# A build-time scheduler's table of priorities: the first six head pairs, the first MLP and the groups of decoded weights get numbers of their own

## The chip, the core and the metric

The kernel runs on one core of a Trainium2 chip. Its work is shared by the TensorE (PE in the profile; PEld is its weight load), VectorE (DVE), ScalarE (ACT), GpSimd (POOL) and SyncE (SP, which here issues most of the DMAs). The metric is the device time in microseconds. The time before is the median of three runs; one further execution was profiled, and every time of an instruction below comes from that one.

## The reference

Attention over 8 batches of 8 heads, and on its output a gated MLP with a product along the sequence. All is fp32.

```python
# q, k, v: (8, 8, 576, 64)
q_rot, k_rot = rotate(q), rotate(k)              # rotary positions
scores = (q_rot @ k_rot.T) / sqrt(64)
attn = exp(scores - max(scores))
out = (attn / (sum(attn) + 1e-9)) @ v
x = out.transpose(0, 2, 1, 3).reshape(8, 576, 512)
h = maximum(x @ w_in, 0)                         # w_in: 512 x 1024
u, v = h[..., :512], h[..., 512:]
v_n = (v - mean(v)) / sqrt(var(v) + 1e-6)
gated = u * (w_spatial @ v_n + b_spatial)        # w_spatial: 576 x 576
result = gated @ w_out                           # w_out: 512 x 512
```

## The kernel before, in words

**Units of work.** Two heads of one batch are a pair; there are 32 pairs, four to a batch. After the pairs 4b to 4b+3 comes the MLP of batch b. Large products are done in several passes with a high and a low part of each operand.

**A pair.** `prepare(i)` loads q and k as `st<i>_0` and `st<i>_1` and applies the rotary positions: two products of 128x576 with the table `tab2` and a sum, on POOL for most pairs (L563, L578). From pair 4 on ACT then scales the k half (`st<i>_1`, L652), DVE makes its low part `lk` (L540), ACT and POOL make `hq` and `lq`, and SP copies all of it by DMA into the stacks `ks`, `qs` and `qz` that the score matmuls read (L429). There is one set of stacks, so those of pair i+1 can be written only when the tiles of pair i that read them are through. `attention(i)` makes nine score tiles `sc<i>_<c>` in the order 0, 1, 2, 3, 8, 4, 5, 6, 7 (four or six matmuls of 288 columns each, L750); DVE takes the negated maximum (`nmx`, L760), ACT the exponential `e` with its sum (L761), DVE transposes it (`tu`, L771), and PE multiplies with v in three pieces of 96 small matmuls (`pv`, L715). `normalise` divides (`rb`, L825, L826) and makes the parts of `x`.

**An MLP.** PE runs `pa` (the v half of the first product, L874), `pb` (the u half, L897), `pc` (along the sequence, L915) and `pd` (the output, L935). `norm` is the normalisation, `gate` the product with u. The weights arrive as 64-bit words and are made into floats by `decode`, once, during the first pairs.

**What sets the order.** Every step is handed to `Program` with the engine it runs on, an estimated length, what it reads and writes, and a sort key. `Program.run` walks through a simulated time at build: whenever an engine is free it takes the ready step with the smallest key, if the buffers that the step opens can be had from their pools (two score tiles `sc`, four `pm` for the MLP's products, four `e`, four `stage`, ...). What comes out is one fixed order of instructions for each engine; on the chip each engine works through its own in order and waits where data isn't there. Where PE would find nothing before 200 us of that simulated time, `warm` matmuls on zeros are put in. The key of a step is 20 times its pair's number (or 80 times its MLP's, plus a start) and an offset from the tables at the top of the file:

```python
PREP = [...]     # offsets of a pair's preparation: load, rope, sum, hi, lo, stacks
STAGE = [...]    # scores, step, max, exp, turn, chunk, values
NORM = [...]     # inverse, fetch, x, its parts
DEC_ON = -60.279479                   # the later steps of a weight's decoding
K_LOAD, K_ROPE, K_SUM, K_HIQ, K_LOQ, K_LOK, K_STACK, K_STACK2 = PREP_E if i < FIRST else PREP
```

`PREP_E`, `STAGE_E` and `NORM_E` hold for the first six pairs together (`FIRST = 6`). An offset thus moves a kind of step against all others, on its engine, without touching what the step does.

Of the kernel before, what the change touches and what calls it, by code (L numbers as in the profile page):

```python
# [22 lines left out]
HF = DFF // 2  # L23
# [6 lines left out]
PE, ACT, DVE, POOL, DMA = "pe", "act", "dve", "pool", "dma"  # L30
# [8 lines left out]
}  # L39
PSUM = {"sc": 1024, "pm": 512}  # L40
MOE_START, MOE_LENGTH = 94.478379, 78.548222
DEC_V = [97.949631, 82.361107, 593.702782, 288.768656]
DEC_S = [84.682668, 152.53349, 99.527247]
DEC_U = [-568.813081, -65.866382, -0.431134, 175.381419]
# [31 lines left out]
K_LATE = 163.209501  # L76
UNTIL = -5282.532269
LATE_LOAD = 300
SOON = 108.92456
FIRST = 6  # L80
PREP = [-848.367164, -374.753764, -69.9844, -244.721214, -617.60192, -1064.500205, 581.882473, -475.784363]
PREP_E = [51.687636, 298.661164, 17.879536, 140.254064, -184.884171, 639.680467, 73.636456, 484.33577]
PREP_AT = [-441.032351, -69.597063, -819.530327, -30.251418, -111.190708, 107.347515]
STAGE = [-7.255147, 1.255075, -127.272341, -353.119135, 244.349862, 3.682899, 10.320485]
STAGE_E = [-17.885167, 1.413295, -324.778667, -335.590414, -18.444203, 500.740646, 14.840595]
ATT_AT = [-7.442792, -9.232278, -6.449832, 1.846545, -111.323694, -67.478676]
NORM = [-413.12016, 513.410815, -713.32848, 231.181969, -280.547004]
NORM_E = [-178.78421, 267.172514, -208.498036, -240.944501, -239.600932]
MOE0 = [106.701094, 81.129356]
# [15 lines left out]
def pool_ns(n):  # L105
    return 160 + n * 32 // 15
# [21 lines left out]
class Program:  # L128
# [5 lines left out]
    def op(self, eng, ns, key, f, r=(), w=(), new=(), port=False, late=0):  # L134
        return self.either({eng: ns}, key, lambda e: f(), r, w, new, port, late)
# [171 lines left out]
def tile_attention_gated_mlp(  # L307
# [11 lines left out]
    nc = tc.nc  # L319
# [23 lines left out]
    op = prog.op  # L343
# [90 lines left out]
    def rest_lo(eng, lo, src, hi):  # L434
        eng.tensor_tensor(out=lo, in0=src, in1=hi.bitcast(F32), op=ALU.subtract)  # L435
# [4 lines left out]
    def decode(key, where, at, src, after=()):  # L440

        n = f"w{'io'[where is wout]}" + "".join(map(str, at))
        tiles = {}
        sg = Buf("m", [P, HF], I32, f"sg{n}")
        tok = ("raw", n)
        ts = nc.vector.tensor_scalar
        stt = nc.vector.scalar_tensor_tensor

        def word(j, dt=None):
            w = tiles["raw"][:, :, j]  # L450
            return w.bitcast(dt) if dt else w
# [392 lines left out]
    def mlp(b):  # L844
        x = xs[4 * b:4 * b + 4]
        pm_pools = "pm"
        start, length = (MOE_START, MOE_LENGTH) if b else MOE0
        base = 80 * b + start
        spent = [0]
        whole = (4 * 12 + 8) * pe_ns(HF) + (16 * 12 + 8 * 14) * pe_ns(HALF)  # L850
# [52 lines left out]
        for f in range(4):  # L903
            fs = slice(f * P, (f + 1) * P)
            for c in range(2):
                pm = Buf(pm_pools, None, None, f"pc{b}_{f}{c}")
                cc = slice(c * HALF, (c + 1) * HALF)
                for t in range(NQ):
# [87 lines left out]
    def gate(u, g, c, pm, key, done):  # L996
# [113 lines left out]
```

## Time and profile before

| what | value |
|---|---|
| median of 3 runs | 897.56 us (893.99 to 898.61) |
| profiled execution: time, and span from its first to its last instruction | 891.51 us, 889.7 us |
| mean granted clock of PE | 0.992 |
| PE busy, matmuls | 858.7 us, 97% of the span |
| PE busy, weight loads | 757.9 us, 85% |
| DVE / ACT / POOL busy | 580.6 us (65%) / 497.5 us (56%) / 511.2 us (57%) |
| share of the chain that ended last: PE / DMA / "issue" | 65% / 11% / 9% |

PE's busy time counts the modelled ends of pipelined matmuls and also a matmul that runs at half clock. So the idle time between groups of weight loads (PEld) is the better place to see PE wait. The profiled execution's own time is 6.05 us below the median.

### The profile page before, as it was taken

The page shows a single profiled execution, that of the slowest core. Times are in us where ns is not written, and L with a number is a line of the kernel's source. Part 1 is how long each engine was busy: PE and PEld are TensorE (multiplying, and loading weights), DVE is VectorE, ACT ScalarE, POOL GpSimd, SP SyncE. Part 2 cuts the span into 40 slices and gives each one's busy share as a digit, 9 for nine tenths or more (in the row PEclk, how much of TensorE's full clock was granted, in tenths as well). Part 3 has the DMA queues.
Part 4 walks back from the last instruction along what each step waited for, and adds up shares of the span by engine and source line. Part 5 has one row for each costly group of instructions (what it writes and reads, how often), then busy time and mean ns, then how long its engine had stood idle before and what let it go on. Part 6 is the DMA issues. An engine that isn't in the chain of part 4 may idle for free.

```text
span 889.7 us, 32677 instructions
## 1 busy us (share of the span) xinstructions
PE 858.7 (97%) x13709; PEld 757.9 (85%) x13709; DVE 580.6 (65%) x1169; ACT 497.5 (56%) x1239; POOL 511.2 (57%) x509
## 2 busy tenths in 40 slices
PE   9999989988999999999999999999999999999998
PEld 7666668878878998889979988899978998899898
DVE  6787788747577665857678565857687665855120
ACT  2665578635448545754558445755567555753442
POOL 7666699766357665566457664566557664312121
PEclk9998899999999999999999999999999999999999
DMA  9977646778888888877888788878987888552101
GB/s 195 246 231 188 146 104 150 174 166 190 211 175 187 189 182 213 190 175 173 210 204 193 171 179 211 186 173 187 224 200 176 187 197 205 121 115 53 54 1 55
DMA packets 99622, 150.88 MB, mean 170 GB/s; under 512 B 30929, under 2 KB 46929, under 8 KB 99474
## 3 DMA queue, kind: packets, MB, share of 16 engines
q1 hardware_dynamic: 98962, 148.12, 71.6%
q8 instruction: 108, 1.77, 0.9%
q10 hardware_dynamic: 512, 0.66, 0.3%
q14 instruction: 40, 0.33, 0.1%
HBM read 94.24 MB, written 9.88 MB: 117 GB/s over the span
## 4 chain that ended last, share of the span: by engine, by line
PE 65%; DMA 11%; issue 9%; SPq 4%; DVE 4%; POOL 4%; ACT 2%; POOLq 0%; DVEq 0%; ACTq 0%
PE sc L750 15%; PE pv L715 11%; PE pc L915 11%; PE pb L897 9%; PE pa L874 7%; PE pd L935 5%; DMA st<-in_qk_dram 4%; PE warm L1009 4%; SPq L429 3%; DMA ks<-st 2%; POOL st L563 2%; PE pr L616 1%; DMA vr<-in_v_dram 1%; DVE tu L771 1%; DVE nmx L760 1%
## 5 line engine op out<-in xcount | busy, mean ns | idle before, releaser
L760 DVE TENSOR_REDUCE nmx<-sc 128x1 f32<-128x576 f32 x288 | 211.5, 740 | 133.5 <-PE sc L750 131.2
L761 ACT ACTIVATE e<-sc,nmx 128x576 f32<-128x576 f32 x288 | 212.5, 739 | 144.7 <-DVE nmx L760 142.5
L771 DVE STREAM_TRANSPOSE tu<-e 128x576 f32<-128x576 f32 x288 | 216.5, 762 | 17.7 <-ACT e L761 9.7
L563 POOL TENSOR_TENSOR st<-st,tab 128x576 f32<-128x576 f32 x112 | 157.8, 1429 | 58.2 <-DMA st<-in_qk_dram 43.5
L715 PE MATMUL pv<-tu,vr 32*64 32x144 f32 x9216 | 177.4, 288 | 11.2 <-issue 11.2
L715 PEld LDWEIGHTS pv<-tu,vr 32*64 32x64 f32 x9216 | 147.9, 131 | 35.8 <-issue 31.8
L750 PE MATMUL sc<-ks,qs 128*128 128x288 f32 x560 | 120.9, 305 | 10.8 <-DVE rb L826 4.3
L915 PE MATMUL pc<-wsp,vn 128*128 128x288 f32 x768 | 126.2, 299 | 0.0
L874 PE MATMUL pa<-wi,x 128*128 128x512 f32 x448 | 118.6, 396 | 0.2 <-DVE rb L825 0.2
L897 PE MATMUL pb<-x,wi 128*128 128x288 f32 x768 | 117.5, 297 | 0.9 <-ACT vv L973 0.8
L935 PE MATMUL pd<-g,wo 128*128 128x288 f32 x744 | 113.6, 297 | 0.0
L915 PEld LDWEIGHTS pc<-wsp,vn 128*128 128x128 f32 x768 | 109.6, 189 | 3.6 <-issue 3.6
L750 PEld LDWEIGHTS sc<-ks,qs 128*128 128x128 f32 x560 | 88.9, 189 | 27.3 <-ACT e L761 8.8
L897 PEld LDWEIGHTS pb<-x,wi 128*128 128x128 f32 x768 | 107.0, 188 | 5.2 <-issue 2.6
L750 PE MATMUL sc<-lk,qz 128*128 128x288 f32 x504 | 108.3, 296 | 0.4 <-issue 0.4
L435 POOL TENSOR_TENSOR vn<-vv,vn 128x512 fp32r<-128x512 f32 (+1 forms) x40 | 51.4, 1292 | 98.9 <-ACT vn L432 98.6
L935 PEld LDWEIGHTS pd<-g,wo 128*128 128x128 f32 x744 | 102.9, 188 | 3.8 <-issue 3.6
L435 POOL TENSOR_TENSOR x<-rb,x 128x64 fp32r<-128x64 f32 (+1 forms) x96 | 59.4, 652 | 79.9 <-ACT x L432 79.9
L874 PEld LDWEIGHTS pa<-wi,x 128*128 128x128 f32 x448 | 79.1, 188 | 14.7 <-issue 1.8
L435 POOL TENSOR_TENSOR g<-u,g 128x288 fp32r<-128x288 f32 x64 | 51.1, 804 | 58.2 <-ACT g L432 58.2
L578 POOL TENSOR_TENSOR st<-st 128x576 f32<-128x576 f32 x56 | 80.0, 1429 | 2.9
L750 PEld LDWEIGHTS sc<-lk,qz 128*128 128x128 f32 x504 | 81.1, 189 | 0.7 <-issue 0.7
(144 smaller groups left out, 897.3 us busy)
## 6 DMA issues: line engine op xcount, KB each, us to landing
vr<-in_v_dram SPq DMA_DIRECT2D x128, 320.0 KB, 7.3
st<-in_qk_dram SPq DMA_DIRECT2D x58, 288.0 KB, 4.9
ks<-st SPq DMA_DIRECT2D x112, 144.0 KB, 4.9
st<-in_qk_dram SPq DMA_DIRECT2D x58, 256.0 KB, 5.1
qs<-hq SPq DMA_DIRECT2D x56, 164.0 KB, 4.0
qs<-lq SPq DMA_DIRECT2D x56, 164.0 KB, 3.8
out_dram<-ob SPq DMA_DIRECT2D x31, 288.0 KB, 3.1
qz<-hq SPq DMA_DIRECT2D x28, 164.0 KB, 6.8
```

Source lines behind the costliest of these rows:

```text
L435: eng.tensor_tensor(out=lo, in0=src, in1=hi.bitcast(F32), op=ALU.subtract)
L563: f = lambda e: e.tensor_tensor(out=st[j][:, cols], in0=st[j][:, cols], in1=tab2[:, cols], op=ALU.mult)
L578: f = lambda e: e.tensor_tensor(out=st[j][:, :S], in0=st[j][:, :S], in1=st[j][:, S:2 * S], op=ALU.add)
L715: nc.tensor.matmul(outs[g][64 * a:64 * a + 64], lhsT=vr[rows, NQ * (at % 4) + at // 4, a, :], rhs=tu[rows, kb, Q4 * a:Q4 * a + Q4], start= ...
L750: nc.tensor.matmul(pt[:, n_c * 512:n_c * 512 + HALF], lhsT=lhsT, rhs=rhs[:, n_c * HALF:n_c * HALF + HALF], start=(n == 0), stop=(n == len( ...
L760: op(DVE, 749, key + k_max, lambda: nc.vector.tensor_reduce(out=nmx.tile, in_=tops(pt), op=ALU.max, axis=AX.XY, negate=True), r=[pt], w=[n ...
L761: op(ACT, 920, key + k_exp, lambda: nc.scalar.activation(e.tile.rearrange("p (c n) -> p c n", c=2), tops(pt), AF.Exp, bias=nmx.tile, scale ...
L771: nc.vector.transpose(out=dst, in_=src)
L874: nc.tensor.matmul(pm[:, :HF], lhsT=lhsT, rhs=win[1, d][:, j, :], start=(d == 0 and n == 0), stop=(d == 3 and n == len(todo) - 1))
L897: nc.tensor.matmul(pm[:, :HALF], lhsT=win[0, d][:, i, f * P:(f + 1) * P], rhs=x[d][:, at:at + HALF], start=(d == 0 and n == 0), stop=(d == ...
L915: nc.tensor.matmul(pm[:, :HALF], lhsT=lhsT, rhs=rhs, start=(t == 0 and n == 0), stop=(t == 4 and n == 1))
L935: nc.tensor.matmul(pm[:, :HALF], lhsT=wout[d,][:, i, m * P:(m + 1) * P], rhs=gs[d][:, at:at + HALF], start=(d == 0 and n == 0), stop=(d == ...
```

## The change

No step is added or taken away and no step is written differently. The tables get other numbers, and some are split: `PREP_E`, `STAGE_E` and `NORM_E` become one row for each of the first six pairs, the constants of `gate` and its neighbours get a second set for the first MLP, and `DEC_ON` becomes one number for each of three groups of weights.

```diff
-DEC_ON = -60.279479
+DEC_G = [659.940102, 469.453537, -180.636876]
...
-EARLY = -540.962515
-STEAL = 253.677474
+EARLY = -742.618406
+STEAL = -309.703072
...
-STAGE_E = [-17.885167, 1.413295, -324.778667, -335.590414, -18.444203, 500.740646, 14.840595]
+STAGE_0 = [-152.625359, 126.181784, -223.095009, -185.92044, 65.524974, 878.665279, -96.81858]
...
-K_NORM, K_RELU, K_GATE, K_GHI, K_GLO, K_OB, K_OUT = 249.262822, 5.067081, 431.336369, -272.695754, 347.344605, 449.209189, 337.36198
+MOE_K = [225.88958, -30.077949, 443.927616, -280.785934, 327.513035, 409.286193, 314.459996]
+MOE_K0 = [304.195457, -304.802348, 139.457459, 618.507128, 430.396321, 222.372613, 212.345366]
...
+        on = DEC_G[2 if where is wout else 1 - at[0]]
...
-        K_LOAD, K_ROPE, K_SUM, K_HIQ, K_LOQ, K_LOK, K_STACK, K_STACK2 = PREP_E if i < FIRST else PREP
+        K_LOAD, K_ROPE, K_SUM, K_HIQ, K_LOQ, K_LOK, K_STACK, K_STACK2 = (PREP_0, PREP_1, PREP_2, PREP_3, PREP_4, PREP_5)[i] if i < FIRST else PREP
...
-        K_S, K_STEP, K_MAX, K_EXP, K_TURN, K_CHUNK, K_VAL = STAGE_E if i < FIRST else STAGE
+        K_S, K_STEP, K_MAX, K_EXP, K_TURN, K_CHUNK, K_VAL = (STAGE_0, STAGE_1, STAGE_2, STAGE_3, STAGE_4, STAGE_5)[i] if i < FIRST else STAGE
...
+        K_NORM, K_RELU, K_GATE, K_GHI, K_GLO, K_OB, K_OUT = MOE_K if b else MOE_K0
```

What matters is the order that comes out. The new tables lengthen the file, so a step's line number is 16 to 18 higher after the change. The names carry the pair and the tile (`e6_4` is tile 4 of pair 6, `st8_1` the k half of pair 8), and behind them a running number.

ACT, at the end of pair 6's tiles, before the change:

```order
L900 ACTIVATE u0_3_2963<-pb0_31_2916 128x288
L652 ACTIVATE st8_1_2789<-st8_1_2789 128x576
L761 ACTIVATE e6_4_3006,sums0_66<-sc6_4_2973,nmx6_4_2990 128x576
L761 ACTIVATE e6_5_3021,sums0_66<-sc6_5_2999,nmx6_5_3011 128x576
L761 ACTIVATE e6_6_3042,sums0_66<-sc6_6_3023,nmx6_6_3031 128x576
L761 ACTIVATE e6_7_3061,sums0_66<-sc6_7_3036,nmx6_7_3047 128x576
```

and after it:

```order
L918 ACTIVATE u0_3_2965<-pb0_31_2919 128x288
L778 ACTIVATE e6_4_2994,sums0_66<-sc6_4_2967,nmx6_4_2978 128x576
L778 ACTIVATE e6_5_3011,sums0_66<-sc6_5_2988,nmx6_5_3000 128x576
L669 ACTIVATE st8_1_2789<-st8_1_2789 128x576
L778 ACTIVATE e6_6_3034,sums0_66<-sc6_6_3013,nmx6_6_3022 128x576
L778 ACTIVATE e6_7_3051,sums0_66<-sc6_7_3028,nmx6_7_3039 128x576
```

The scaling of pair 8's k half has moved behind the exponentials of tiles 4 and 5. It still stands ahead of those of tiles 6 and 7.

The scaling reads what POOL makes. POOL in the same part of the program, before (the instruction of line 578 is the sum that ends the rope):

```order
L563 TENSOR_TENSOR st8_0_2705<-st8_0_2705,tab2_63 128x576 x2
L563 TENSOR_TENSOR st8_1_2789<-st8_1_2789,tab2_63 128x576
L578 TENSOR_TENSOR st8_0_2705<-st8_0_2705 128x576
L563 TENSOR_TENSOR st8_1_2789<-st8_1_2789,tab2_63 128x576
L435 TENSOR_TENSOR x5_2922<-rb5_2779,x5_2922 128x512
L435 TENSOR_TENSOR x5_2922<-rb5_2779,x5_2922 128x64 x2
L578 TENSOR_TENSOR st8_1_2789<-st8_1_2789 128x576
L563 TENSOR_TENSOR st9_0_2810<-st9_0_2810,tab2_63 128x576 x2
```

and after:

```order
L580 TENSOR_TENSOR st8_0_2706<-st8_0_2706,tab2_63 128x576 x2
L595 TENSOR_TENSOR st8_0_2706<-st8_0_2706 128x576
L451 TENSOR_TENSOR x5_2898<-rb5_2778,x5_2898 128x512
L451 TENSOR_TENSOR x5_2898<-rb5_2778,x5_2898 128x64 x2
L580 TENSOR_TENSOR st8_1_2789<-st8_1_2789,tab2_63 128x576 x2
L580 TENSOR_TENSOR st9_0_2815<-st9_0_2815,tab2_63 128x576
L595 TENSOR_TENSOR st8_1_2789<-st8_1_2789 128x576
L580 TENSOR_TENSOR st9_0_2815<-st9_0_2815,tab2_63 128x576
```

The products for `x5` now come before both products of `st8_1`, and one product of `st9_0` stands between them and the sum of `st8_1`.

PE from the first to the second score tile of pair 6, before:

```order
L750 MATMUL sc6_0_2794<-ks_71,qs_70 128x288 x2
L750 MATMUL sc6_0_2794<-lk6_2643,qz_72 128x288 x2
L897 MATMUL pb0_20_2722<-x1_1349,wi01_1473 128x288 x3
L897 MATMUL pb0_21_2806<-x0_996,wi00_1343 128x288 x3
L897 MATMUL pb0_20_2722<-x2_1653,wi02_1631 128x288 x3
L897 MATMUL pb0_21_2806<-x1_1349,wi01_1473 128x288 x3
L897 MATMUL pb0_20_2722<-x3_2002,wi03_1881 128x288 x3
L897 MATMUL pb0_21_2806<-x2_1653,wi02_1631 128x288 x3
L750 MATMUL sc6_1_2832<-ks_71,qs_70 128x288 x2
```

and after (the line of dots stands for the rest of a `pv5` piece of 96 matmuls):

```order
L767 MATMUL sc6_0_2793<-ks_71,qs_70 128x288 x2
L767 MATMUL sc6_0_2793<-lk6_2711,qz_72 128x288 x2
L915 MATMUL pb0_20_2714<-x2_1647,wi02_1625 128x288 x3
L915 MATMUL pb0_21_2806<-x0_996,wi00_1337 128x288 x3
L915 MATMUL pb0_20_2714<-x3_1996,wi03_1875 128x288 x3
L915 MATMUL pb0_21_2806<-x1_1343,wi01_1402 128x288 x3
L732 MATMUL pv5_0_2635<-tu5_2467,vr5_2469 64x144
...
L767 MATMUL sc6_1_2875<-ks_71,qs_70 128x288 x2
```

The third piece of pair 5's `pv` now stands between the two tiles; before, it came behind the second and six more `pb`. Ahead of the first tile there are now twelve `pb` between two `pv5` pieces, where there were six.

PE from the last tile of pair 7 that reads the first head's stacks (`sc7_8`) to the first tile of pair 8, which needs them written anew, before (35 `pc` and 16 score matmuls lie between `sc7_8` and `sc8_0`):

```order
L750 MATMUL sc7_8_3356<-ks_71,qs_70 128x288 x4
L750 MATMUL sc7_8_3356<-lk7_2777,qz_72 128x288 x2
L750 MATMUL sc7_4_3367<-ks_71,qs_70 128x288 x2
...
L915 MATMUL pc0_31_3429<-wsp_1975,vn_1965 128x288 x3
L750 MATMUL sc7_7_3443<-ks_71,qs_70 128x288 x2
L750 MATMUL sc7_7_3443<-lk7_2777,qz_72 128x288 x2
L915 MATMUL pc0_31_3429<-wsp_1975,vn_1965 128x288 x6
L915 MATMUL pc0_31_3429<-wt1_68,vn_1965 128x288
L915 MATMUL pc0_31_3429<-wt2_69,vn_1965 128x288
L750 MATMUL sc8_0_3471<-ks_71,qs_70 128x288 x2
```

and after (53 `pc`, 16 score matmuls and two warm ones lie between):

```order
L767 MATMUL sc7_8_3322<-ks_71,qs_70 128x288 x4
L767 MATMUL sc7_8_3322<-lk7_2723,qz_72 128x288 x2
L933 MATMUL pc0_20_3315<-wsp_1969,vn_1963 128x288 x3
L933 MATMUL pc0_21_3341<-wsp_1969,vn_1963 128x288 x3
L933 MATMUL pc0_20_3315<-wsp_1969,vn_1963 128x288 x3
L767 MATMUL sc7_4_3353<-ks_71,qs_70 128x288 x2
...
L1028 MATMUL warm_3458<-zero_64 128x256
...
L933 MATMUL pc0_31_3430<-wt1_68,vn_1963 128x288
L933 MATMUL pc0_31_3430<-wt2_69,vn_1963 128x288
L767 MATMUL sc8_0_3474<-ks_71,qs_70 128x288 x2
```

`sc7_8` has moved ahead of 18 `pc`.

## Rows read from the trace of the kernel before

**Rows 1.** The page: busy time, share of the span and instructions of each engine.

```profile
PE 858.7 (97%) x13709; PEld 757.9 (85%) x13709; DVE 580.6 (65%) x1169; ACT 497.5 (56%) x1239; POOL 511.2 (57%) x509
```

**Rows 2.** Windows: us, busy us (x instructions) by engine, PEclk, DMA share, GB/s.

```profile
75.00:100.00 25.00, 23.25 (x515) 15.35 (x522) 18.26 (x32) 13.10 (x31) 12.81 (x13) 0.80 0.70 153
...
150.00:175.00 25.00, 23.33 (x416) 21.79 (x417) 19.74 (x40) 17.12 (x43) 19.97 (x20) 1.00 0.81 182
175.00:200.00 25.00, 20.65 (x384) 18.81 (x382) 13.07 (x23) 10.50 (x28) 17.85 (x18) 0.93 0.78 170
200.00:225.00 25.00, 22.74 (x373) 21.10 (x368) 17.01 (x30) 13.09 (x32) 17.52 (x18) 1.00 0.80 181
...
300.00:400.00 100.00, 97.61 (x1678) 89.10 (x1660) 67.93 (x141) 59.10 (x148) 61.99 (x59) 1.00 0.85 193
```

**Rows 3.** Timeline of the weight loads (PEld), 176 to 186 us: start, length, idle before.

```profile
178.48 1.25 PEld L915 LDWEIGHTS pc<-wsp,vn 128*128 128x128 f32 x9
182.31 0.50 PEld L750 LDWEIGHTS sc<-ks,qs 128*128 128x128 f32 x2 [2.59 <-ACT e L761]
```

**Rows 4.** Timeline of ACT, 176 to 187 us.

```profile
180.86 0.68 ACT L652 ACTIVATE st<-st 128x576 fp32r<-128x576 f32 x1 [2.97 <-POOL st L578]
181.45 0.72 ACT L761 ACTIVATE e<-sc,nmx 128x576 f32<-128x576 f32 x1
```

**Rows 5.** Timeline of POOL, 176 to 185 us.

```profile
177.62 1.85 POOL L435 TENSOR_TENSOR x<-rb,x 128x512 fp32r<-128x512 f32 x3
179.42 1.41 POOL L578 TENSOR_TENSOR st<-st 128x576 f32<-128x576 f32 x1
180.78 2.79 POOL L563 TENSOR_TENSOR st<-st,tab 128x576 f32<-128x576 f32 x2
```

**Rows 6.** Windows over the two stretches at half clock, columns as in rows 2.

```profile
83.30:93.40 10.10, 10.10 (x54) 5.32 (x60) 4.87 (x8) 3.94 (x11) 8.59 (x10) 0.50 0.89 192
182.30:185.60 3.30, 3.28 (x13) 3.29 (x14) 2.22 (x3) 1.52 (x4) 2.68 (x2) 0.50 0.60 134
```

**Rows 7.** Timeline of the weight loads (PEld), 161 to 169 us.

```profile
164.21 0.30 PEld L750 LDWEIGHTS sc<-ks,qs 128*128 128x128 f32 x2 [0.95 <-issue]
...
168.37 0.30 PEld L750 LDWEIGHTS sc<-ks,qs 128*128 128x128 f32 x2 [1.19 <-ACT e L761]
```

**Rows 8.** Timeline of DVE, 158 to 169 us.

```profile
159.12 2.99 DVE L540 SCALAR_TENSOR_TENSOR lk<-st 128x576 fp32r<-128x576 f32 x1
...
164.32 0.76 DVE L540 SCALAR_TENSOR_TENSOR lk<-st 128x576 fp32r<-128x576 f32 x1
```

**Rows 9.** Timeline of POOL, 156 to 169 us.

```profile
160.00 1.50 POOL L578 TENSOR_TENSOR st<-st 128x576 f32<-128x576 f32 x1
```

**Rows 10.** Timeline of the weight loads (PEld), 203 to 214 us.

```profile
203.87 0.32 PEld L750 LDWEIGHTS sc<-lk,qz 128*128 128x128 f32 x2
...
209.85 0.85 PEld L915 LDWEIGHTS pc<-wsp,vn 128*128 128x128 f32 x6
210.65 0.32 PEld L915 LDWEIGHTS pc<-wt,vn 128*128 128x128 f32 x2
212.67 0.30 PEld L750 LDWEIGHTS sc<-ks,qs 128*128 128x128 f32 x2 [1.69 <-ACT sums L781]
```

**Rows 11.** Timeline of SP's queue (SPq), 190 to 213 us: DMA issues.

```profile
203.93 1.28 SPq L429 DMA_DIRECT2D ks<-st  x2
...
206.53 0.59 SPq L429 DMA_DIRECT2D qs<-lq  x1
```

**Rows 12.** Chain that ended last, 155 to 215 us: start, length, what.

```profile
168.35 4.92 DMA st<-in_qk_dram
...
190.96 1.71 PE pv L715 x96
...
206.53 5.13 DMA qs<-lq
```

**Rows 13.** Waits of PE, whole run: waiter, releaser, us in total, times, longest.

```profile
PE pv L715 <- issue: 11.2, 13, 1.7
```

More of the change, by code (lines that the diff above doesn't have):

```diff
@@ L41 @@
 MOE_START, MOE_LENGTH = 94.478379, 78.548222
-DEC_V = [97.949631, 82.361107, 593.702782, 288.768656]
-DEC_S = [84.682668, 152.53349, 99.527247]
-DEC_U = [-568.813081, -65.866382, -0.431134, 175.381419]
-DEC_ON = -60.279479
+DEC_V = [48.648717, 298.484594, 589.774644, 512.781613]
+DEC_S = [236.652718, 275.818517, 334.039505]
+DEC_U = [-681.183786, 87.093253, 231.078998, 554.683933]
+DEC_G = [659.940102, 469.453537, -180.636876]
 PLAIN = 4
@@ L50 @@
 KPE, QPE = TURNED, TURNED
-K_V = [27.234326, 64.747493]
-DEC_O = [113.18323, -246.5008, -70.36556, -68.947851]
+K_V = [109.861511, -113.641373]
+DEC_O = [307.509008, -573.199219, 123.9321, 42.10241]
 NB = S // 32
@@ L90 @@
-K_NORM, K_RELU, K_GATE, K_GHI, K_GLO, K_OB, K_OUT = 249.262822, 5.067081, 431.336369, -272.695754, 347.344605, 449.209189, 337.36198
+PREP = [-888.918029, -387.686371, -101.675055, -242.200332, -611.967582, -1035.506748, 527.353178, -486.008321]
+PREP_0 = [275.82189, 79.988984, -283.22331, -119.214795, -507.386783, 781.127013, 134.877372, 0.627105]
+PREP_1 = [41.307893, 16.274961, 645.735259, 84.951737, -332.204651, 623.290832, 415.003064, 252.792244]
+PREP_2 = [-9.316576, 263.797731, -55.856231, -255.14748, -179.536651, 928.724309, 664.072014, 103.773633]
@@ new lines @@
+PREP_3 = [110.497314, 310.444141, -102.132977, 162.612523, 391.082226, 761.33236, 272.497405, 615.024291]
+PREP_4 = [-317.537533, 415.637985, 325.563548, -147.832255, 161.233426, 234.006917, 544.234268, 725.641855]
+PREP_5 = [46.204584, 594.87858, -89.473906, 417.283725, 606.492232, 970.232725, 479.452256, 451.065018]
+PREP_AT = [-684.542266, -114.433201, -790.930628, -239.427645, -268.857947, -183.879065]
+STAGE = [-7.579453, 1.27644, -178.511844, -361.191028, 221.245646, 3.581157, 10.341775]
@@ new lines @@
+STAGE_0 = [-152.625359, 126.181784, -223.095009, -185.92044, 65.524974, 878.665279, -96.81858]
+STAGE_1 = [-930.307299, 92.605123, -717.610591, -491.842258, -599.850806, 503.158235, 22.890267]
+STAGE_2 = [-21.057236, 2.789288, -1347.72468, -511.877354, 8.255286, 730.363442, 28.853901]
+STAGE_3 = [-21.664391, 12.612128, -330.835719, -231.918175, -385.365694, 1249.119114, -84.177922]
+STAGE_4 = [-499.357067, 60.843447, -413.786987, 328.721182, 252.944368, 478.781929, 106.205233]
+STAGE_5 = [1.358468, 20.420333, -559.384946, -671.036707, 357.425815, 64.415035, 268.880017]
@@ new lines @@
+ATT_AT = [-5.219765, -23.575078, -20.902619, -35.96937, -295.354852, -236.296969]
+NORM = [-487.408952, 522.405141, -785.812451, 202.230656, -275.735301]
+NORM_0 = [-225.092449, 157.761179, 621.843386, -270.186805, -320.963245]
+NORM_1 = [-1084.535816, 744.498527, -43.693383, -359.285786, 346.264313]
+NORM_2 = [-297.654847, 153.832544, -739.029766, -227.639472, -98.764723]
+NORM_3 = [-694.126339, -244.756737, -388.611612, -420.733027, -176.776499]
+NORM_4 = [-316.381535, 961.222033, -342.871301, 62.983705, -40.105664]
@@ L472, in decode @@
         op(DVE, 640, key, bits(20, 0x7FF, ALU.logical_shift_right, ALU.bitwise_and), r=[t1, *after], w=[pt], new=[pt])
-        op(ACT, 600, key - DEC_ON, lambda: nc.scalar.activation(ints(), ints(), AF.Relu, bias=bias, scale=float(2**23)), r=["bias"], w=[pt])
-        op(DVE, 640, key - DEC_ON, lambda: stt(out=sg.tile, in0=word(1), scalar=-(2**31), in1=ints(), op0=ALU.bitwise_and, op1=ALU.bitwise_or), r=[t1, pt], w=[sg], new=[sg])
-        op(DVE, 640, key - DEC_ON, lambda: ts(out=ints(), in0=word(1), scalar1=0xFFFFF, scalar2=None, op0=ALU.bitwise_and), r=[t1], w=[pt])
@@ L476, in decode @@
-        op(ACT, 500, key - DEC_ON, lambda: nc.scalar.activation(pt.tile, ints(), AF.Copy, bias=1.0, scale=2.0**-20), w=[pt])
-        op(DVE, 640, key - DEC_ON, lambda: stt(out=val.tile, in0=word(0, U32), scalar=2.0**-52, in1=pt.tile, op0=ALU.mult, op1=ALU.add), r=[t0, pt], w=[val], new=[val])
+        op(ACT, 600, key - on, lambda: nc.scalar.activation(ints(), ints(), AF.Relu, bias=bias, scale=float(2**23)), r=["bias"], w=[pt])
+        op(DVE, 640, key - on, lambda: stt(out=sg.tile, in0=word(1), scalar=-(2**31), in1=ints(), op0=ALU.bitwise_and, op1=ALU.bitwise_or), r=[t1, pt], w=[sg], new=[sg])
@@ L479, in product @@
+        op(DVE, 640, key - on, lambda: ts(out=ints(), in0=word(1), scalar1=0xFFFFF, scalar2=None, op0=ALU.bitwise_and), r=[t1], w=[pt])
+        op(ACT, 500, key - on, lambda: nc.scalar.activation(pt.tile, ints(), AF.Copy, bias=1.0, scale=2.0**-20), w=[pt])
+        op(DVE, 640, key - on, lambda: stt(out=val.tile, in0=word(0, U32), scalar=2.0**-52, in1=pt.tile, op0=ALU.mult, op1=ALU.add), r=[t0, pt], w=[val], new=[val])
         def product(e):
             e.tensor_tensor(out=val.tile, in0=val.tile, in1=sg.tile.bitcast(F32), op=ALU.mult)
-        prog.either({POOL: pool_ns(HF), **({DVE: 640} if key - DEC_ON < EARLY else {})}, key - DEC_ON, lambda e: product(vec[e]), r=[sg], w=[val])
@@ L483, in decode @@
-        op(ACT, 480, key - DEC_ON, high, r=[val], w=[t0, t1, (n, "hi")])
-        prog.either({POOL: pool_ns(HF), **({DVE: 640} if key - DEC_ON < EARLY else {})}, key - DEC_ON, lambda e: rest_lo(vec[e], where[at][:, 1, :], val.tile, where[at][:, 0, :]), r=[val, (n, "hi")], w=[n])
+        prog.either({POOL: pool_ns(HF), **({DVE: 640} if key - on < EARLY else {})}, key - on, lambda e: product(vec[e]), r=[sg], w=[val])
+        op(ACT, 480, key - on, high, r=[val], w=[t0, t1, (n, "hi")])
+        prog.either({POOL: pool_ns(HF), **({DVE: 640} if key - on < EARLY else {})}, key - on, lambda e: rest_lo(vec[e], where[at][:, 1, :], val.tile, where[at][:, 0, :]), r=[val, (n, "hi")], w=[n])
@@ L920, in mlp @@
                     key = mm(pe_ns(HALF) * (3 if t < 4 else 2), mul, r=need, w=[pm], new=[pm] if t == 0 else [])
-                gate(us[f], gs[f], c, pm, key, [("gated", b)] if f == 3 and c == 0 else [])
+                gate(us[f], gs[f], c, pm, key, [("gated", b)] if f == 3 and c == 0 else [], (K_GATE, K_GHI, K_GLO))
         for m in range(4):
@@ L994, in norm, with gate @@
             op(POOL, pool_ns(HF), key, port=True, f=lambda: rest_lo(nc.gpsimd, vn(4, 0)[64:P], vv[0:64], vn(4, 0)[0:64]), r=[vv, ("vn", t, 0)], w=[("vn", t, 1)])
-    def gate(u, g, c, pm, key, done):
+    def gate(u, g, c, pm, key, done, ks):
+        K_GATE, K_GHI, K_GLO = ks
         cc = slice(c * HALF, (c + 1) * HALF)
```

22 lines of the change are left out of this document (8 added, 14 removed).

## The prediction

> **What bounds the kernel now.** I read the page first: PE is busy for 858.7 of 889.7 us, and no other engine for more than two thirds [rows 1]. So only what PE waits for, or does at half clock, can be won. Next come the windows, to see where. In a steady hundred microseconds PE is busy for 97.6 and its clock is granted in full; from 175 to 200 it is busy for 20.65 of 25 at a mean clock of 0.93, and from 75 to 100 the clock is 0.80 [rows 2]. The steps of the change are those of the first six pairs, the first MLP and the decoding, so the losses it can reach lie ahead of some 275 us, and the windows say that they are thickest where the first MLP runs beside pairs 6 to 8.
>
> The timelines then name the waits there. At 182.31 the weight load of tile 6 of pair 6 starts after 2.59 us of nothing, released by an exponential on ACT [rows 3]. ACT had itself stood for 2.97 us in front of the scaling of `st8_1`, waiting for POOL's sum; the exponential of tile 4, which freed the score buffer, stands behind it in ACT's row and starts at 181.45 [rows 4]. POOL was doing `x5` and then that sum, to 180.83 [rows 5]. Right behind the wait the granted clock is 0.50 over 182.3 to 185.6 [rows 6], the lower of PE's two levels (1.2 and 2.4 GHz). Before that, tiles 0 and 1 of pair 6 cost 0.95 and 1.19 us [rows 7]. After it, the first tile of pair 8 waits for 1.69 us [rows 10]: SP issues that pair's first copies at 203.93, just as `sc7_8` ends, the low part of q only at 206.53 [rows 11], and that one takes 5.13 us to land [rows 12]. The view names a sum on ACT there, but the chain shows the copy.
>
> **The change, term by term.** The unit is PE's pitch: six `pc` matmuls start at 209.85 and the next group at 210.65, so 0.80 / 6 = 0.133 us for each [rows 10]. A whole `pv` piece of 96 takes 1.71 us [rows 12].
>
> *Tile 6 of pair 6 and the half clock.* With the scaling behind the exponentials of tiles 4 and 5, these no longer wait for POOL, and buffer by buffer tile 6 follows tile 4 and tile 7 follows tile 5. The wait of 2.59 us goes; against the short gaps that every such place has I count 2.5. In the 3.3 us at half clock PE did what takes it half of that at full clock, so 1.65 us more goes if the clock stays up. It had fallen right behind the longest stop of this stretch, and that stop is gone. The bounds are 0 and 2.6 for the wait, 0 and 1.7 for the clock.
>
> *What it costs next.* The scaling still stands ahead of tile 6's exponential, which frees the buffer of `sc7_0`. POOL now does a product of `st9_0` in between, 2.79 / 2 = 1.4 us [rows 5]. The load of `st8_1` lands at 168.35 + 4.92 = 173.27 [rows 12]. Two products, the strange one and the sum, 4 x 1.4 us, put the sum's end at 178.9 at the earliest; the old end and one product more, 180.83 + 1.4 = 182.2, is the latest. Scaling (0.68) and exponential with its sum (some 0.9) end at 180.5 to 183.8. PE, from where it would reach tile 6 (178.48 + 1.25 = 179.7 [rows 3], less 1.9 from the next term, so 177.8), does eight score matmuls and 26 `pc`, 34 x 0.133 = 4.5 us, and asks for `sc7_0` at 182.3. So 0 to 1.5 us comes back here. I take 0.5: the earliest case needs only that `x5` is done when the load lands.
>
> *Tiles 0 and 1 of pair 6.* Six more `pb` ahead of tile 0 are 0.80 us against 0.95. Between the tiles 18 matmuls became 12 and a `pv` piece, 1.71 - 0.80 = 0.91 us more against 1.19. DVE's `lk` for pair 6 took 2.99 us, the next one 0.76 [rows 8]; it ended just behind POOL's sum, which ended at 161.50 [rows 9], and the normalisation of the MLP's last rows queued behind it, then ACT's part of that, then the exponential of tile 0. That work now stands ahead of `lk`. Of 2.14 us I count 1.9, with 0 and 2.1 as bounds.
>
> The Trainium skill (SBUF — State Buffer, Who interferes with whom) says that a DVE instruction with two inputs in SBUF contends with a GpSimd instruction that reads SBUF; rows 8 and 9 agree, with 2.99 us against 0.76. By that rule the moved `lk` may be held again, which is the second rival.
>
> *First tile of pair 8.* Between `sc7_8` and `sc8_0` there were 51 matmuls, 6.8 us; the copies took 212.67 - 204.0 = 8.7. Now there are 69, 9.2 us, and two warm ones. The copies are issued from the same event, so the wait of 1.69 goes, and I count 1.65; bounds 0 and 1.7. SP gets the fetch of pair 6's inverses ahead of a load, not behind it, which moves nothing into this chain.
>
> *The rest.* One rope product of pair 2 goes from POOL to DVE, at a price between 0.76 us, the nearest row of that size on DVE [rows 8], and 1.4 on POOL [rows 5]; PE has warm matmuls there, so I count nothing (0 to 0.7 either way). The decoding's rows shift by a few places under the same cover. PE's row up to pair 4 is the same but for single warm matmuls, so the stretch at half clock of 83.3 to 93.4 [rows 6] stays. From pair 12 on, about twelve score tiles stand three matmuls earlier, 0.4 us each: 0 to 4.8 us lost, if a tile waits for all of it. PE is busy there for 97.6% [rows 2], so most have slack; I take 1.2.
>
> The sum: 2.5 + 1.65 + 1.9 + 1.65 = 7.7 us gained, 0.5 + 1.2 given back, 6.0 net. The profiled execution took 891.51, so it would take 885.5. The median shown is 6.05 above that execution, and against it I forecast 897.56 - 6.0 = 891.5, which is 0.67% faster.
>
> **The rivals.** First, *the wait only moves* from tile 6 to `sc7_0`: POOL runs late, the sum ends near 182.2 and what comes back is 1.5, the clock falls behind that stop as it did before (1.65), and the steady tiles cost 2.5. Then 7.7 - 1.5 - 1.65 - 2.5 = 2 us are left: 895.5. For it speaks that the scaling was not moved behind all four exponentials; against it that PE comes to `sc7_0` 4.5 us after tile 6.
>
> Second, *`lk` is held again.* POOL's row has five products and sums without a pause around it. If it is held for the 2.2 us that rows 8 show and PE waits that long at tile 0, the gain is 6.0 - 2.2 = 3.8: 893.8.
>
> Third, *slower: waits inside `pv`.* Thirteen times PE stood inside a `pv` piece with nothing to wait for that the profile shows, 11.2 us in all, 0.86 each [rows 13]. They come where PE runs through many short instructions, so each place depends on everything in PE's row before it, and the change moves pieces of `pv`. It ends slower, at 902.1 and above, from (902.1 - 891.5) / 0.86 = 12 more such waits on. Against that stands that PE's row from pair 12 on hardly changes. The Trainium skill (Runtime: NRT & Kernel Launch, Instruction fetch mechanics) says that fetching instructions across a block boundary is "mostly hidden"; if these waits are fetches, rows 13 don't bear that out, and by the page this rival would cost nothing.
>
> Fourth, *nothing changes*: small losses at the front, where decoding and pairs 0 to 5 are shuffled, eat the gain. 897.5. Fifth, *the early half clock goes too*: 10.1 us at half clock give back up to 5.05, so 886.5; only warm matmuls and a moved weight step speak for it.
>
> **How the numbers follow.** Chances: the forecast 0.52 (its own range 888 to 894), the moved wait 0.18, `lk` 0.10, slower 0.08, nothing 0.05, the early clock 0.07. The predicted time is the forecast's. The range of 886 to 897 takes in the first two rivals and the fifth; outside are the third, the fourth and the tails. A difference under 0.5% is about what a measurement of this kernel can't tell from no change. Faster by more means below 893.1: 0.48 of the forecast, the early clock, and 0.02 of the second rival, 0.57. Within it are 0.04 of the forecast, the moved wait, 0.08 of `lk` and the fourth, 0.35. Slower is 0.08.
>
> **What would show it.** In the changed kernel's profile: no idle time over 0.5 us ahead of the weight loads of tile 6 of pair 6 and tile 0 of pair 8; a granted clock of 1.00 from 175 to 200; ACT's stop at the scaling still there, but shorter than 2 us and behind tile 5's exponential; `lk` of pair 6 under 1.5 us; `sc7_0` waiting for less than 1 us; pair 9's tiles some 6 us earlier than before, and the same distance at the end. The forecast is wrong if the waits at pair 6 return under other names, if a new stretch at half clock shows up, or if the early gain is lost again in the steady hundreds, which should show a PE busy of 97.5 or more.

## The result and the profile after

The changed kernel takes 897.86 us (median of 20 runs, 893.87 to 904.46), the one before 894.31 (20 runs). The measured ratio is 1.0065, with a 95% interval of 1.0043 to 1.0088: the change makes the kernel slower by 0.65%. (The two medians alone would give 0.40%; the ratio with its interval is what counts here and below.) The prediction said 891.5 and faster by 0.67%; 897.86 lies above its range. The median of three runs of before that it started from, 897.56, was itself 3 us above that of the 20. The profiled execution of the change took 898.12 us.

The windows of the changed kernel, with the columns of [rows 2], and 580 to 590 by itself:

```profile
150.00:175.00 25.00, 23.08 (x416) 21.56 (x415) 17.39 (x40) 16.33 (x41) 22.49 (x22) 1.00 0.82 182
175.00:200.00 25.00, 18.95 (x371) 17.31 (x369) 11.67 (x20) 10.70 (x26) 17.55 (x16) 0.93 0.78 166
200.00:225.00 25.00, 23.17 (x343) 21.89 (x343) 16.45 (x30) 12.60 (x32) 13.28 (x15) 1.00 0.84 187
...
500.00:600.00 100.00, 94.98 (x1591) 87.28 (x1579) 67.09 (x138) 56.94 (x144) 57.45 (x55) 0.98 0.79 181
```

```profile
580.00:590.00 10.00, 9.82 (x62) 9.83 (x63) 8.89 (x18) 7.51 (x19) 3.32 (x5) 0.83 1.06 225
```

Two things are to be seen. From 175 to 200, where 2.5 us of waiting and the half clock should have gone, PE is busy for less than before and the clock is the same 0.93. And there is a new hole between 500 and 600, in the steady part, with 95.0 us of PE work and a clock of 0.98. Before, that stretch was:

```profile
500.00:600.00 100.00, 98.17 (x1687) 89.35 (x1686) 67.49 (x140) 57.81 (x147) 59.01 (x57) 1.00 0.81 187
```

Some 2 us of the missing 3.2 are one stop inside a `pv`, which ends at 502.9. The traces of the experiments front12 and vr6, which have before's order there, show that stop too (1.75 and 1.71 us), so the change isn't its cause. The rest, and the clock, are the second place below.

The first place, in the changed kernel's timeline of the weight loads, of ACT and of SP's queue, and in its chain:

```profile
181.76 0.32 PEld L933 LDWEIGHTS pc<-wt,vn 128*128 128x128 f32 x2
185.79 0.50 PEld L767 LDWEIGHTS sc<-ks,qs 128*128 128x128 f32 x2 [3.71 <-issue]
```

```profile
179.49 0.69 ACT L669 ACTIVATE st<-st 128x576 fp32r<-128x576 f32 x1 [0.61 <-POOL st L595]
180.08 0.72 ACT L778 ACTIVATE e<-sc,nmx 128x576 f32<-128x576 f32 x1
```

```profile
169.98 2.37 SPq L445 DMA_DIRECT2D vr<-in_v_dram  x4
174.00 1.15 SPq L445 DMA_DIRECT2D ks<-st  x2
175.25 0.54 SPq L445 DMA_DIRECT2D qs<-hq  x1
175.88 1.11 SPq L445 DMA_DIRECT2D qz<-hq  x1
177.09 0.54 SPq L445 DMA_DIRECT2D qs<-lq  x1
```

```profile
177.09 8.50 DMA qs<-lq
...
205.06 8.47 DMA qs<-lq
```

ACT does what was forecast: its stop is down from 2.97 us [rows 4] to 0.61, POOL's sum ends at 179.46, and tile 6's exponential runs at 180.08. Tile 6 doesn't wait any more. But tile 0 of pair 7 does, for 3.71 us, and not for an exponential: the last copy into pair 7's first stacks was issued at 177.09 and lands at 185.59. In front of these copies stands the load of a pair's v, four times 320 KB. Before, the last of them was issued at 178.69. PE then stood at tile 6 to 182.31, ran at half clock to 185.6, came to tile 0 of pair 7 at 187.36 and didn't wait there:

```profile
178.69 0.46 SPq L429 DMA_DIRECT2D qs<-lq  x1
```

```profile
187.36 0.32 PEld L750 LDWEIGHTS sc<-ks,qs 128*128 128x128 f32 x2
```

The wait on ACT, with the half clock behind it, had covered a wait on DMA. The experiment act6 below shows that by itself.

The second place is the order of SP, which my prediction had not read there. SP's queue before, and then after the change:

```profile
564.31 0.59 SPq L429 DMA_DIRECT2D qs<-lq  x1
565.00 0.53 SPq L429 DMA_DIRECT2D rt21d<-rt  x1
565.97 0.49 SPq L411 DMA_DIRECT2D st<-in_qk_dram  x1
...
567.16 1.60 SPq L414 DMA_DIRECT2D st<-in_qk_dram  x1
568.92 1.92 SPq L429 DMA_DIRECT2D rb<-rt21d  x3
```

```profile
565.74 0.59 SPq L445 DMA_DIRECT2D qs<-lq  x1
567.30 0.49 SPq L427 DMA_DIRECT2D st<-in_qk_dram  x1
...
568.49 1.80 SPq L430 DMA_DIRECT2D st<-in_qk_dram  x1
570.34 0.59 SPq L445 DMA_DIRECT2D rt21d<-rt  x1
573.08 2.21 SPq L445 DMA_DIRECT2D rb<-rt21d  x3
```

The inverses of a pair's sums go out to memory (`rt21d`) and come back spread over the partitions (`rb`). The put stood right behind the stacks' copies, with the load of pair 24's k half between put and fetch; now it stands behind that load. Before, issuing the load filled the time from put to fetch; now SP stands for 2.15 us between them, and the issue of the fetch ends at 575.29. At no other pair from 10 on does the put change its place. (From pair 12 on SP's row differs in two more ways: pair 22's v stands ahead of the load of pair 25, and in five MLPs a copy into a stack stands ahead of an output store.) The changed kernel's timelines of DVE and of the weight loads show who waits for the fetch:

```profile
579.23 0.52 DVE L842 TENSOR_TENSOR rb<-pv,rb 128x144 f32<-128x144 f32 x2 [2.68 <-DMA rb<-rt21d]
```

```profile
580.17 0.30 PEld L767 LDWEIGHTS sc<-ks,qs 128*128 128x128 f32 x2 [2.21 <-DVE rb L843]
```

It is tile 3 of pair 22. Before, DVE waited there too, but PE did not:

```profile
574.95 0.52 DVE L825 TENSOR_TENSOR rb<-pv,rb 128x144 f32<-128x144 f32 x2 [2.07 <-DMA rb<-rt21d]
```

```profile
575.89 0.30 PEld L750 LDWEIGHTS sc<-ks,qs 128*128 128x128 f32 x2
```

### The profile page after: what moved, and what is told of

Same layout as the page of the kernel before. It is cut to its first block, busy times and chain, and to the rows that moved or that the text cites. A ratio compares the mean times of both kernels' runs of the same rounds, so it can differ in the third digit from the quotient of the medians.

```text
span 896.3 us, 32685 instructions
## 1 busy us (share of the span) xinstructions
PE 859.4 (96%) x13710; PEld 760.0 (85%) x13710; DVE 576.3 (64%) x1170; ACT 499.6 (56%) x1239; POOL 513.4 (57%) x508
## 4 chain that ended last, share of the span: by engine, by line
PE 60%; DMA 15%; issue 8%; SPq 6%; POOL 5%; DVE 4%; ACT 2%; ACTq 0%; DVEq 0%; POOLq 0%
PE sc L767 15%; PE pc L933 11%; PE pv L732 10%; PE pb L915 9%; PE pa L892 7%; PE pd L953 4%; SPq L445 4%; DMA qs<-lq 2%; POOL st L580 2%; DMA vr<-in_v_dram 2%; PE warm L1028 2%; DMA st<-in_qk_dram 1%; DMA wst<-in_w_spT_dram 1%; DMA qs<-hq 1%; DVE tu L788 1%
## 5 line engine op out<-in xcount | busy, mean ns | idle before, releaser
L915 PE MATMUL pb<-x,wi 128*128 128x288 f32 x768 | 120.1, 299 | 0.6 <-DVE rb L842 0.4
```

The source lines that it names most:

```text
L915: nc.tensor.matmul(pm[:, :HALF], lhsT=win[0, d][:, i, f * P:(f + 1) * P], rhs=x[d][:, at:at + HALF], start=(d == 0 and n == 0), stop=(d == ...
```

## The experiments

For these kernels the scheduler doesn't choose. Each engine's order was taken down as a list from either kernel, and the list is played back. So one row can be moved and all others stay. Line numbers are higher by the length of the lists. No kernel plays back before's own order with nothing moved. That playing back has no price of its own is taken from front12, vr6 and act6vr6, all within 0.2% of before. One thing is not kept apart: the buffers come to lie partly at other addresses. Of the kernels below, rest12, p21, sp21, oth21, sp17, getfirst and act6 share one placement, and all seven come out slower than before.

```diff
-                    item = heapq.heappop(ready[e])
...
+                k = order[e][0]
...
+                    chosen = self.ops[k]
+                    if chosen.waits or not place(chosen.new):
+                        continue
...
+                order[e].pop(0)
```

There are many points at which both orders have done the same set of steps, and from one such point to the next a kernel can have either order. Each ratio below is to the kernel before on the same chip, five rounds, with its 95% interval. To place a loss I also matched PE's order with each trace, and give the time from tile 0 of pair 22 to tile 0 of pair 23: 25.6 us before, 28.6 after the change.

**Where the loss is.** Front from the one, rest from the other:

```diff
 # front12: the change to the start of pair 12, then before;  rest12: the other way round
 # p21: before, but the change from pair 20 to 22;  no21: the change, but before from pair 20 to 22
```

front12. 

> Each engine's order is that of the change up to the start of pair 12's tiles, and that of before from there on. Copy theory: pair 6 and pair 8 wait for their stacks' copies whatever ACT does, so the front is worth nothing either way: ratio to before 0.998 to 1.002, and tile 0 of pair 7 waits 2 us or more with a mean clock below 1.00 from 175 to 200 us. Front theory (the loss comes from the first twelve pairs): ratio 1.005 to 1.009. The prediction's own theory would want 0.993 to 0.996.

rest12. 

> Each engine's order is that of before up to the start of pair 12's tiles, and that of the change from there on. Theory of the late put (SP issues pair 21's inverses behind a load, tile 3 of pair 22 waits for them): ratio to before 1.003 to 1.007, with a wait of about 2 us at tile 3 of pair 22 and a granted clock below 1.00 behind it. Front theory: ratio 0.998 to 1.002.

p21. 

> Before's order everywhere but from pair 20 to pair 22, where each engine has the change's order. Theory of the late put: this stretch alone costs 3 to 4 us, ratio to before 1.003 to 1.005, and the same wait and clock show as in the whole change. Theory of a spread loss (small waits inside the value products all over the program, because PE's row is shifted): ratio 0.999 to 1.002.

no21. 

> The change's order everywhere but from pair 20 to pair 22, where each engine has before's order. Theory of the late put: most of the loss is gone, ratio to before 1.000 to 1.003. Front theory or spread loss: ratio 1.005 to 1.008.

Measured: front12 0.9995 (0.9977 to 1.0013) and 25.3 us; rest12 1.0081 (1.0051 to 1.0111) and 30.0; p21 1.0071 (1.0040 to 1.0102) and 28.0; no21 1.0007 (0.9985 to 1.0029) and 26.2. Tile 0 of pair 7 waits for 3.54 us in front12 and 4.00 in no21. So the front is worth nothing that can be measured, and the stretch of pairs 20 to 22 holds the loss: 206 of 4118 steps, counted on each engine from the first row that differs to the last. rest12 and p21 lose more than I had expected. At tile 3 of pair 22 PE stands for 3.60 us in rest12 and 2.93 in p21, but p21 keeps a clock of 1.00 behind it.

**One row of SP's order.**

```diff
 # sp21 (from before); sp17 is the same with rt17d and st20_1
-DMA rt21d<-rt21
 DMA st24_1<-in_qk_dram
+DMA rt21d<-rt21
 # fix21 and fix21b (from the change): the row back ahead of st24_1
 # oth21 (from before): pairs 20 to 22 as in the change on PE, ACT, DVE, POOL; SP as before
```

sp21. 

> Before, with one row of SP's order moved: the put of pair 21's inverses comes behind the load of pair 24's k half instead of ahead of it. Nothing else is changed. Theory of the late put: this row alone makes the wait at tile 3 of pair 22 (2 us or more, behind the fetch of the inverses), the time from tile 0 of pair 22 to tile 0 of pair 23 grows from some 25.7 to 28 us or more, ratio 1.003 to 1.007. Rival (it is the order of PE, ACT and DVE in that stretch that costs, SP's only follows): ratio 0.998 to 1.002 and no such wait.

fix21. 

> The change, with the put of pair 21's inverses moved back ahead of the load of pair 24's k half in SP's order, and nothing else. Theory of the late put: ratio to before 0.999 to 1.003, the wait at tile 3 of pair 22 under 1.2 us. Rival (the other engines' order in that stretch): ratio 1.004 to 1.008.

sp17. 

> Before, with the put of pair 17's inverses moved behind the load of pair 20's k half in SP's order: the same move as in sp21, four pairs earlier. If the late put costs by its place in a period of four pairs, it is the same here: tile 3 of pair 18 waits 2 us or more, ratio 1.003 to 1.008. If pair 21 was peculiar: ratio 0.999 to 1.002.

oth21. 

> Before, and from pair 20 to pair 22 the change's order on PE, ACT, DVE and POOL, but before's on SP: p21 without its late put. If the put alone costs, the ratio to before is 0.998 to 1.002 and pair 22 takes 25 to 26 us from its tile 0 to that of pair 23. If the other engines' order costs too (fix21 left 1.0034), the ratio is 1.002 to 1.005.

fix21b. 

> The kernel fix21 again, for its interval of 1.0012 to 1.0056 leaves open whether the put is the whole loss. If it is, the ratio comes out at 0.999 to 1.002; if the rest of the stretch costs, at 1.002 to 1.005.

Measured: sp21 1.0074 (1.0052 to 1.0097). The weight loads and DVE in sp21:

```profile
583.50 0.30 PEld L877 LDWEIGHTS sc<-ks,qs 128*128 128x128 f32 x2 [3.40 <-DVE rb L953]
```

```profile
582.57 0.52 DVE L952 TENSOR_TENSOR rb<-pv,rb 128x144 f32<-128x144 f32 x2 [5.46 <-DMA rb<-rt21d]
```

One put behind one load, in before's surroundings, loses as much as the whole change. sp17 makes it 1.0043 (1.0015 to 1.0071): there the wait falls on a `pb`, whose buffer the same `rb` frees, and not on tile 3 as expected:

```profile
480.08 0.74 PEld L1025 LDWEIGHTS pb<-x,wi 128*128 128x128 f32 x3 [3.33 <-DVE rb L952]
```

Taking the put back does not take back all: some half of the change's 0.65% is left. fix21 is 1.0034 (1.0012 to 1.0056), fix21b 1.0035 (1.0008 to 1.0061), though tile 3 of pair 22 has no wait over 0.4 us in either and the stretch takes 25.2 and 25.1 us. Both keep pair 22's v ahead of the load of pair 25, which no21 doesn't; no kernel moves that row alone. oth21, which I expected to settle that, is the slowest of these, 1.0100 (1.0067 to 1.0134), and loses in another place. SP's queue in oth21:

```profile
572.21 1.92 SPq L555 DMA_DIRECT2D rb<-rt21d  x3
582.37 0.49 SPq L537 DMA_DIRECT2D st<-in_qk_dram  x1
...
584.25 1.96 SPq L555 DMA_DIRECT2D vr<-in_v_dram  x4
586.30 1.15 SPq L555 DMA_DIRECT2D ks<-st  x2
```

SP stands from 574.1 to 582.4 at a load of pair 25, and behind it are v of pair 22 and pair 23's stacks; the change has that v ahead of the load. Pair 23 then waits four times, 0.95 to 0.98 us each, and takes 27.5 us to pair 24's tile 0, where all other kernels take 24.2 to 26.0. So SP's order and that of the engines go together, and oth21 doesn't say what the engines' order costs alone.

**The load between put and fetch.** In getfirst the load, that of the pair three on, stands behind the fetch at four pairs of before:

```diff
 DMA rt13d<-rt13
-DMA st16_1<-in_qk_dram
 DMA rb13<-rt13d
+DMA st16_1<-in_qk_dram
```

> Before, with the load of the k half four pairs on moved behind the fetch of the inverses at pairs 13, 17, 21 and 25 (it stood between put and fetch). If the fetch is late because the load is ahead of it, the wait at tile 3 of these pairs' tiles (0.7 to 1.1 us each, behind the previous pair's fetch) is not touched, and that of the next pair has slack; SP now stands at the fetch until the put has landed, and everything behind it is later by some 2 us. Theory of slack: ratio 0.998 to 1.002. If every microsecond of SP's order counts: slower by 1 us or more for each place, ratio 1.004 to 1.010. If the fetch's place is what binds: ratio 0.994 to 0.998.

Measured: 1.0251 (1.0219 to 1.0283), the slowest of all and more than twice the loss of my worst case. ACT and the weight loads in getfirst:

```profile
385.29 0.68 ACT L779 ACTIVATE st<-st 128x576 fp32r<-128x576 f32 x1 [6.79 <-DMA vr<-in_v_dram]
385.88 0.72 ACT L888 ACTIVATE e<-sc,nmx 128x576 f32<-128x576 f32 x1
```

```profile
386.75 0.50 PEld L877 LDWEIGHTS sc<-ks,qs 128*128 128x128 f32 x2 [5.61 <-ACT e L888]
```

The load lands late, POOL's sum with it (383.86 to 385.26), ACT stands at the scaling, and tile 5 of pair 14 waits for an exponential behind it. The view names a copy of v as releaser; the sum's end says it was POOL. It is the stop of [rows 4] again, at three of the four places with 5.5 to 5.9 us on PE.

**Pair 7's stacks.** Two rows of before, alone and together:

```diff
 # act6, on ACT                      # vr6, on SP; act6vr6 has both
-ACTIVATE st8_1<-st8_1              -DMA vr6<-in_v_dram
 ACTIVATE e6_4                       DMA ks<-st7_1, qs<-hq, qz<-hq, qs<-lq
 ACTIVATE e6_5                      +DMA vr6<-in_v_dram
+ACTIVATE st8_1<-st8_1
 # frontvr: front12 with v of pairs 6 and 7 behind the stacks of pairs 7 and 8
```

act6. 

> Before, with one row of ACT's order moved: the scaling of pair 8's k half stands behind the exponentials of tiles 4 and 5 of pair 6, as in the change. Copy theory: the wait at tile 6 goes (2.5 us or more to under 0.5), and tile 0 of pair 7 waits 2 us or more instead, for the copy of q's low part, which lands at the same time as before: ratio 0.998 to 1.002, clock from 175 to 200 us still below 1.00. The prediction's theory: ratio 0.994 to 0.997 and a full clock.

vr6. 

> Before, with only the load of pair 6's v moved behind the copies into pair 7's first stacks (ACT's order as before). Copy theory: ACT still makes tile 6 of pair 6 wait for 2.5 us or more, so PE comes to tile 0 of pair 7 no sooner: ratio 0.997 to 1.002. Together with act6 and act6vr6 this shows two limits one behind the other.

act6vr6. 

> As act6, and in SP's order the load of pair 6's v (four copies of 320 KB) stands behind the copies into pair 7's first stacks instead of ahead of them. Copy theory: those copies no longer queue behind 1.3 MB, land 3 to 5 us sooner, and tile 0 of pair 7 waits under 1 us: ratio 0.993 to 0.997. Rival (the copies are slow by themselves, whatever stands ahead): the wait stays, ratio 0.998 to 1.002. If v now lands late, the first value product of pair 6 waits.

frontvr. 

> The change's order up to the start of pair 12's tiles, before's from there on, and in SP's order the loads of v of pairs 6 and 7 moved behind the copies into the first stacks of pairs 7 and 8. Copy theory: the waits at tile 0 of pair 7 (3.5 us) and of pair 8 (1.6) go to under 1 us each, the clock from 175 to 200 us is full, and since the change has pair 6's inverses put ahead of a load the wait of the kernel act6vr6 at tile 8 of pair 7 doesn't come: ratio to before 0.991 to 0.996. Rival (DMA as a whole bounds pairs 6 to 9, so that a saved wait comes back a pair later): ratio 0.997 to 1.001.

The first wait of each in the weight loads, act6, then vr6, then act6vr6:

```profile
187.43 0.50 PEld L877 LDWEIGHTS sc<-ks,qs 128*128 128x128 f32 x2 [4.86 <-issue]
```

```profile
186.51 0.30 PEld L877 LDWEIGHTS sc<-ks,qs 128*128 128x128 f32 x2 [4.36 <-ACT e L888]
```

```profile
183.22 0.30 PEld L877 LDWEIGHTS sc<-ks,qs 128*128 128x128 f32 x2 [0.89 <-ACT e L888]
...
201.93 0.98 PEld L877 LDWEIGHTS sc<-ks,qs 128*128 128x128 f32 x4 [2.45 <-issue]
```

With ACT's row moved, tile 0 of pair 7 waits for the copies, the last of which lands at 187.26; with SP's moved, tile 6 of pair 6 still waits for ACT; with both, tile 0 of pair 7 waits for 0.89 us and the clock from 175 to 200 is full. The issues' times to landing, act6 from 171 to 180 us and act6vr6 from 172 to 178:

```profile
ks<-st SPq DMA_DIRECT2D x2, 144.0 KB, 9.4
```

```profile
ks<-st SPq DMA_DIRECT2D x2, 144.0 KB, 2.8
```

So the copies are slow because of the v ahead of them. But the times hardly move: vr6 0.9991 (0.9964 to 1.0018), act6vr6 1.0014 (0.9987 to 1.0040), act6 even 1.0042 (1.0019 to 1.0065). In act6vr6 the next wait is there already: 2.45 us at tile 8 of pair 7, since DVE waits for pair 6's inverses, put behind a load in before's order:

```profile
200.93 0.52 DVE L952 TENSOR_TENSOR rb<-pv,rb 128x144 f32<-128x144 f32 x2 [2.47 <-DMA rb<-rt6d]
```

frontvr, which has that put ahead of the load, comes to tile 0 of pair 8 at 207.1 us, where before comes at 212.7. Of these 5.6 us won 2.5 are left at tile 0 of pair 10. The weight loads of frontvr:

```profile
215.40 1.57 PEld L842 LDWEIGHTS pv<-tu,vr 32*64 32x64 f32 x94 [2.00 <-ACT ob L1066]
...
220.96 1.73 PEld L842 LDWEIGHTS pv<-tu,vr 32*64 32x64 f32 x85 [2.86 <-issue]
```

The first of these waits is for ACT, and ACT for a copy into pair 8's second stacks. The chain and ACT's timeline in frontvr:

```profile
206.82 6.71 DMA qz<-hq
```

```profile
213.55 0.78 ACT L558 ACTIVATE hq<-st 128x512 fp32r<-128x512 f32 x2 [3.24 <-DMA qz<-hq]
```

Moved behind the first stacks' copies, v stands right ahead of the second stacks', and these are late now. The second wait is a stop inside `pv`, of which more below. frontvr's ratio is 0.9986 (0.9959 to 1.0013): the fastest of all, and not told apart from before.

## Why the prediction was wrong

Two steps failed. The front was to gain 7.2 us net, and front12 measures nothing: its interval goes from 2.1 us faster to 1.2 us slower. The steady part was to lose 1.2 us, and it holds the whole loss.

**The rest of the sum.** The step that failed for the sign is the one on the steady part, 1.2 us for "about twelve score tiles" that "stand three matmuls earlier" (by the two orders it is 26 tiles, three of them by nine matmuls). I had compared PE's row from pair 12 on and not SP's. One put moved behind one load there, and that alone brings the wait and a loss (sp21). The same prediction had weighed that kind of move for pair 6, in the other direction, at nothing. How much of the loss is the put's is less sure. sp21 measures 0.74%, 6.6 us on 894.9. The traces place about half of that: the four kernels with the late put take 28.0 to 30.4 us for pair 22, mean 29.2, before 25.6. And in the change itself, taking the put back is worth some 0.3% (1.0065 against fix21's 1.0034). For the other half of sp21's loss the placement of its buffers is a rival that no run excludes, since act6 has the same placement and loses 0.42% with no late put.

**Tile 6 and the half clock.** "The wait of 2.59 us goes" was right, and so was that ACT's scaling was late behind POOL. The forecast of what is late next was wrong: 0 to 1.5 us for tile 6's exponential, 3.71 us measured for a copy by DMA. (On its way to `sc7_0` PE has 22 `pc` and not the 26 counted, 4.0 us and not 4.5; that changes little.) The rows that told it, the stacks' copies of [rows 11] and the 5.13 us of [rows 12], I had read for pair 8 and not asked for pair 7. The clock fell behind that stop as it had behind the other.

**First tile of pair 8.** "The copies are issued from the same event, so the wait of 1.69 goes": it is 1.96 in the trace after:

```profile
213.74 0.30 PEld L767 LDWEIGHTS sc<-ks,qs 128*128 128x128 f32 x2 [1.96 <-ACT g L448]
```

PE had some 9 us of work in between as forecast, but the copies took longer. The last was issued at 205.06, 1.5 us earlier than before, and landed at 213.53 (the view names ACT, the chain shows this copy). It took 8.47 us, where [rows 12] give 5.13 for before and PE's start at 212.67 allows 6.1 at most. Ahead of it stands the same load of v; its issue began 2.0 us before the first copy's, where it had been 3.8.

**Tiles 0 and 1 of pair 6** went as the sum had it in part. `lk` took 0.79 us and not 2.99, so the second rival didn't come, though POOL was at work beside it without a pause (157.82 to 161.30). The tiles are reached 1.4 and 1.1 us earlier, and 0.75 us stays at tile 1. It was won for nothing, since the stacks decide behind it.

```profile
158.94 0.79 DVE L557 SCALAR_TENSOR_TENSOR lk<-st 128x576 fp32r<-128x576 f32 x1
```

```profile
167.35 0.30 PEld L767 LDWEIGHTS sc<-ks,qs 128*128 128x128 f32 x2 [0.75 <-ACT e L778]
```

**The rivals.** The first, that the wait only moves, was right on the place (`sc7_0`) and on the front's result, though not on the mechanism. The third named the right sign for a wrong reason: PE's waits inside `pv` are about what they were, by the row of after that answers to [rows 13]:

```profile
PE pv L732 <- issue: 12.4, 11, 2.3
```

What these stops are the traces do show. The 16 kept traces, before's among them, hold 38 stops of PE inside `pv` pieces of over 1.5 us between 125 and 870 us. In 37 a transfer of 16 KB of the instruction queue lands during the stop, 1.3 to 1.6 us before PE goes on; the one without is the stop that ACT ended in frontvr. This says that PE waits there for its own instructions.

The early half clock stayed.

What stays open: why fix21 keeps 0.3% where no21 has none measurable, with intervals that overlap (pair 22's v on SP and the other engines' order in that stretch are what differs); and why act6 is slower, whose one trace is 4.3 us ahead of before's at tile 0 of pair 24 and loses 6 us from there to pair 27, in an order that is before's.

## What to carry to other kernels

A wait that ends last may cover another one of the same length; before counting it as won, look when everything else that the waiter needs would have been there. Where one queue issues all transfers in order, compare that queue's order row by row over the whole program: a small put that someone waits for must not stand behind a load that isn't urgent, and the large load behind a small urgent copy, if its own user has the time and no other urgent copy comes next (in frontvr one did). A search over a table of priorities can be taken apart by playing back its orders piece by piece, which here led to one row out of thousands that alone makes the wait; and putting that row back, which won only half, shows why both directions have to be run.

## What the runs showed of the hardware

Copies of 144 KB took 2.8 us to land with no load of v ahead of them and 9.4 us behind 1.3 MB of it: most of such a copy's time to landing was here what had been issued ahead of it, from the same queue. In 37 stops of 1.5 to 2.9 us inside `pv` pieces a 16 KB transfer of the instruction queue landed shortly before PE went on. And the lower clock (1.2 GHz) followed long stops of PE behind ACT (2.59 us in before) as behind DMA (3.71 us after the change), but not each: p21 stood for 3.27 us at tile 6 of pair 6 and kept a clock of 1.00 from 175 to 200.
